# Other idle products and 18 idle elementwise operations behind the last product of a Fourier, mixer and channel-MLP kernel

## The chip, the cores and the metric

The kernel runs on one core of one Trainium2 chip. The metric is device time in microseconds (us) of one execution; a kernel's time is the median of several runs. The core has a matrix engine (TensorE, PE in the profile, with PEld for its weight loads), three elementwise engines (VectorE: DVE, ScalarE: ACT, GpSimd: POOL), SyncE (SP), which here only starts DMAs, and 16 DMA engines. [...]

## The reference

```python
def _attn_ref(x, w_r, w_i, b_r, b_i):            # x: 8 x 3136 x 256
    X = np.fft.rfft(x, axis=1)
    Yr = Xr @ w_r - Xi @ w_i + b_r
    Yi = Xr @ w_i + Xi @ w_r + b_i
    # soft threshold by 0.01 on Yr and Yi
    ...
    return np.fft.irfft(Y, n=x.shape[1], axis=1)

def _moe_ref(x, U, V, w_ch1, w_ch2):
    xt = x.transpose(0, 2, 1)
    h = xt @ U @ V                               # tokens, rank 32
    u = x + h.transpose(0, 2, 1)
    ch = np.maximum(u @ w_ch1, 0.0) @ w_ch2      # 256 -> 1024 -> 256
    return u + ch
```

The output is `_moe_ref` of `_attn_ref`, in fp32.

## The kernel before

The Fourier transforms of length 3136 = 49 x 64 are products with constant matrices, in stages over 8 batches. PSUM tiles are named after their stage: `psa` and `psb` transform, `psq` and `pst` mix the channels, `psc` and `psd` transform back, `psu`, `psp` and `psv` belong to the rank-32 token product. The channel MLP then runs over 49 windows of 512 tokens: `psx`, `psy` and `psz` hold its first layer, `pso0` and `pso1` its second. Most operands are split into a high and a low part (names ending in h and l) and multiplied in three products of type fp32r; VectorE, ScalarE and GpSimd make the splits, sums and ReLUs.

The work is recorded as a list of operations, and a planner (`_Program.order`) sets the order of each engine from costs and due times. `prog.trace` then issues them, so that each recorded operation has line 517 (the call in `trace`), whatever it is. Each engine runs its list in order; a wait is for a semaphore count of another engine or of its own. The last recorded operations are the second-layer products of window 47 (`pso`), two additions `xq<-xq,pso` and two transposes `os<-xq` on VectorE, one pair for each half of the 256 channels, and four DMAs `out_dram<-os`, two from SyncE and two from ScalarE.

Behind all of that, in program order, `more_idle` issues products whose results nobody reads. Before the change it issues on TensorE alone: 56 products over three PSUM tiles `psidle_0` to `psidle_2`, all with weights and columns out of `w1t`, a constant tile of 128 x 7168 fp32r values (the first layer's weights). They read 512 columns contiguously (5 with 128, 5 with 72 columns of weights), with a step of two (5), in pairs 256 columns apart (5), one pair again and again (5), in halves of the array (64 rows: 8 of 512, 8 of 256 columns and 6 of 64 in fp32), in quarters of it (64 rows and 64 weight columns: 4 of 256, in fp32), and shifted by one column (5). An fp32 product appears as two records in the trace, an fp32r product as one, so that 56 products are 66 records. Their line is 526, in the helper `mm`.

The name before `<-` in a row of the profile is the tile written, the names behind it the tiles read; `128x512` is partitions by elements.

Of the kernel before, what the change touches and what calls it, by code (L numbers as in the profile page):

```python
# [13 lines left out]
F32 = mybir.dt.float32  # L14
F32R = mybir.dt.float32r
U32 = mybir.dt.uint32
AF = mybir.ActivationFunctionType
ALU = mybir.AluOpType
# [498 lines left out]
            call(*[real(a) for a in op.args], **{k: real(a) for k, a in op.kw.items()})  # L517


def more_idle(nc, pool, w):  # L520

    o = [pool.tile([128, 512], F32, tag=f"psf.{k}", bufs=1, name=f"psidle_{k}") for k in range(3)]
    lhsT = w[:, 4096:4224]

    def mm(out, lhsT, rhs):
        nc.tensor.matmul(out, lhsT=lhsT, rhs=rhs, start=True, stop=True, skip_group_check=True)  # L526

    two = w[:, 0:1024].rearrange("p (n t) -> p t n", t=2)
    cross = w[:, 0:512].rearrange("p (t n) -> p n t", t=2)
    same = w[:, 0:2].unsqueeze(1).broadcast_to([128, 256, 2])  # L530
    for _ in range(5):
        mm(o[0], lhsT, w[:, 0:512])
    for _ in range(5):
        mm(o[0][:72], w[:, 4096:4168], w[:, 0:512])
    for _ in range(5):
        mm(o[0], lhsT, two[:, 0])
    for _ in range(5):
        mm(o[0].rearrange("p (n t) -> p n t", t=2), lhsT, cross)
    for _ in range(5):
        mm(o[0].rearrange("p (n t) -> p n t", t=2), lhsT, same)  # L540
    for n in (512, 256):
        for k in range(8):
            r = 64 * (k % 2)
            mm(o[1 + k % 2][:, :n], w[r : r + 64, 4096:4224], w[r : r + 64, 0:n])
    f = w.bitcast(F32)
    for k in range(6):
        r = 64 * (k % 2)
        mm(o[1 + k % 2][:, :64], f[r : r + 64, 4096:4224], f[r : r + 64, 0:64])
    for k in range(4):
        r, c = 64 * (k // 2), 64 * (k % 2)  # L550
        mm(o[1 + k // 2][c : c + 64, :256], f[r : r + 64, 4096:4160], f[r : r + 64, 0:256])
    for _ in range(5):
        mm(o[0], lhsT, w[:, 1:513])


@with_exitstack
def fft_mix_moe_kernel(
# [19 lines left out]
    nc = tc.nc  # L577
    prog = _Program()
    act, dve, pool, pe, dma = [prog.engine(e) for e in ("act", "dve", "pool", "pe", "sp")]
    const, dram = _Pool("const", 1), _Pool("dram", 1, "dram")  # L580
    ps_f, ps_m, ps_o = _Pool("ps_f", 3, "psum"), _Pool("ps_m", 1, "psum"), _Pool("ps_o", 1, "psum")
    fp, qp, mp = _Pool("fp", 2), _Pool("qp", 2), _Pool("mp", 1)
# [41 lines left out]
    w1t = const.tile([128, 7, 2, 512], F32R, name="w1t", tag="w1")  # L624
# [1078 lines left out]
    for w, prev, next_w in zip(turn_w, [None] + turn_w, turn_w[1:] + [None]):  # L1703
        b, j = divmod(w, NW)
# [18 lines left out]
        for g in range(2):  # L1723
            l1s = l1_chunks(w, g)
            new = l2_chunks(w, g)
            for k in range(4):
                for c in range(2):
                    n = WS * j + 8 * g + 2 * k + c
# [26 lines left out]
    make_identity(nc, ident.get())  # L1755
    with tc.manual_schedule():
        prog.trace(engines, ident.get())
        more_idle(nc, ps_f.real, w1t.get().rearrange("p a b c -> p (a b c)"))


def _dft_constants():
# [81 lines left out]
```

## Time and profile before

| | us |
|---|---|
| runs | 1695.21, 1695.93, 1697.87 |
| median | 1695.93 |
| profiled execution, its own time | 1696.02 |
| profiled execution, span | 1693.9 |
| mean granted TensorE clock | 1.000 |

The span runs from the first to the last instruction of the profiled execution, and its own time is 2.1 us longer. Times in a row of the timeline count from the start of the span. A row of the page's groups reads: line, engine, operation, tiles, shapes, count, then total busy us and mean ns of one, then the idle time of the engine before them and what ended it. A row of one tile's view has min, median and max ns of one, and the first and last start in us. A row of the timeline has start, length and what, and in brackets the idle time before it and its releaser; neighbours of one form are merged, with their count. Products are pipelined: the next starts before the last one ends, so that the step from start to start is shorter than one product's length.

### The profile page before, as it was taken

The page shows a single profiled execution, that of the slowest core. Times are in us where ns is not written, and L with a number is a line of the kernel's source. Part 1 is how long each engine was busy: PE and PEld are TensorE (multiplying, and loading weights), DVE is VectorE, ACT ScalarE, POOL GpSimd, SP SyncE. Part 2 cuts the span into 40 slices and gives each one's busy share as a digit, 9 for nine tenths or more (in the row PEclk, how much of TensorE's full clock was granted, in tenths as well). Part 3 has the DMA queues.
Part 4 walks back from the last instruction along what each step waited for, and adds up shares of the span by engine and source line. Part 5 has one row for each costly group of instructions (what it writes and reads, how often), then busy time and mean ns, then how long its engine had stood idle before and what let it go on. Part 6 is the DMA issues. An engine that isn't in the chain of part 4 may idle for free.

```text
span 1693.9 us, 31590 instructions
## 1 busy us (share of the span) xinstructions
PE 1685.3 (99%) x11170; PEld 1517.5 (90%) x11170; DVE 1323.8 (78%) x2487; ACT 1015.1 (60%) x2187; POOL 574.9 (34%) x502
## 2 busy tenths in 40 slices
PE   9999999999999999999999999999999999999999
PEld 6979989999898999999988989999989999998888
DVE  6798898589856989678866788768985689766774
ACT  4766776466665765456666666555666566554442
POOL 2312553133533443133344444123343233211221
DMA  9863444223653444313464344422465233410221
GB/s 256 243 225 92 139 124 129 86 80 108 173 163 109 129 141 118 110 51 89 133 198 124 118 142 112 133 69 73 118 167 160 63 104 104 119 59 18 69 66 26
DMA packets 243448, 200.64 MB, mean 118 GB/s; under 512 B 131386, under 2 KB 192608, under 8 KB 243292
## 3 DMA queue, kind: packets, MB, share of 16 engines
q1 hardware_dynamic: 240654, 197.77, 40.5%
q8 instruction: 89, 1.46, 0.4%
q10 hardware_dynamic: 2638, 0.86, 0.2%
q14 instruction: 67, 0.55, 0.1%
HBM read 121.36 MB, written 77.20 MB: 117 GB/s over the span
## 4 chain that ended last, share of the span: by engine, by line
PE 97%; DMA 2%; DVE 1%; ACT 0%; POOL 0%; issue 0%; SPq 0%; DVEq 0%
PE pso L517 32%; PE psy L517 18%; PE psx L517 8%; PE psq L517 7%; PE psd L517 7%; PE psb L517 5%; PE psa L517 5%; PE psz L517 4%; PE psc L517 4%; PE pst L517 4%; PE psv L517 1%; PE psidle L526 1%; DMA xx<-in_x_dram 0%; DMA fb<-in_fb_dram 0%; DMA zt<-zd 0%; DMA fas<-in_fa_dram 0%
## 5 line engine op out<-in xcount | busy, mean ns | idle before, releaser
L517 PE MATMUL pso<-rh,w2t 128*128 128x512 f32 x1568 | 433.5, 398 | 0.0
L517 PEld LDWEIGHTS pso<-rh,w2t 128*128 128x128 f32 x1568 | 275.3, 188 | 44.8
L517 PE MATMUL pso<-rl,w2t 128*128 128x512 f32 x784 | 246.7, 396 | 0.0
L517 DVE SCALAR_TENSOR_TENSOR ys<-tb,rl 64x256 f32<-64x256 f32 x350 | 197.3, 564 | 12.2 <-ACT rl L517 6.8
L517 POOL TENSOR_TENSOR yl<-ys,yh 128x512 fp32r<-128x512 f32 (+1 forms) x101 | 136.8, 1354 | 190.7 <-ACT yh L517 173.1
L517 POOL TENSOR_TENSOR xl<-xt,xh 98x512 fp32r<-98x512 f32 x96 | 130.6, 1360 | 204.7 <-ACT xh L517 190.4
L517 PEld LDWEIGHTS pso<-rl,w2t 128*128 128x128 f32 x784 | 147.4, 188 | 35.3
L517 DVE SCALAR_TENSOR_TENSOR rl<-s,rh 128x512 fp32r<-128x512 f32 x196 | 156.5, 805 | 5.1 <-ACT rh L517 2.9
L517 ACT ACTIVATE rh<-s 128x512 fp32r<-128x512 f32 x196 | 121.6, 629 | 57.6 <-DVE s L517 56.3
L517 POOL TENSOR_TENSOR tl<-ts,th 128x256 fp32r<-128x256 f32 x88 | 71.0, 806 | 203.8 <-ACT th L517 144.2
L517 PE MATMUL psq<-wmt,xsh 128*128 128x256 f32 (+1 forms) x704 | 130.3, 282 | 0.0
L517 PE MATMUL psy<-odh,w1t 128*128 128x256 f32 x784 | 126.2, 283 | 0.0
L517 DVE TENSOR_TENSOR v<-v,psy 128x512 f32<-128x512 f32 x98 | 67.1, 685 | 72.9 <-ACT v L517 63.1
L517 PEld LDWEIGHTS psy<-odh,w1t 128*128 128x128 f32 x784 | 113.5, 189 | 10.0
L517 PEld LDWEIGHTS psq<-wmt,xsh 128*128 128x128 f32 (+1 forms) x704 | 112.0, 188 | 5.3 <-issue 0.2
L517 PE MATMUL psd<-dt,zt 98*128 98x130 f32 x896 | 115.0, 275 | 0.5 <-DMA dt<-dud 0.5
L517 PEld LDWEIGHTS psd<-dt,zt 98*128 98x128 f32 x896 | 110.9, 190 | 4.6 <-issue 0.7
L517 ACT ACTIVATE xsh<-psb 128x256 fp32r<-128x256 f32 (+1 forms) x176 | 60.5, 381 | 89.7 <-PE psb L517 87.4
L517 ACT ACTIVATE xq<-psd 128x196 f32<-128x196 f32 x256 | 82.0, 332 | 48.0 <-PE psd L517 37.3
L517 DVE TENSOR_TENSOR pa<-pa,psd 128x64 f32<-128x64 f32 x248 | 54.1, 218 | 68.1 <-ACT xq L517 59.1
L517 ACT ACTIVATE v<-psx 128x512 f32<-128x512 f32 x98 | 58.6, 598 | 76.8 <-PE psx L517 67.3
L517 POOL TENSOR_TENSOR ocl<-xq,och 128x256 fp32r<-128x256 f32 x47 | 37.8, 804 | 195.0 <-ACT och L517 194.9
(217 smaller groups left out, 4296.0 us busy)
## 6 DMA issues: line engine op xcount, KB each, us to landing
zt<-zd SPq DMA_DIRECT2D x128, 196.0 KB
zd<-zs SPq DMA_DIRECT2D x192, 128.0 KB
out_dram<-os SPq DMA_DIRECT2D x190, 128.0 KB
t<-gd SPq DMA_DIRECT2D x168, 128.0 KB
xt<-in_x_dram SPq DMA_DIRECT2D x100, 196.0 KB
gd<-gs SPq DMA_DIRECT2D x96, 196.0 KB
fb<-in_fb_dram SPq DMA_DIRECT2D x96, 128.0 KB
vw<-vd SPq DMA_DIRECT2D x96, 128.0 KB
```

The lines of the kernel that those rows point to most:

```text
L517: call(*[real(a) for a in op.args], **{k: real(a) for k, a in op.kw.items()})
L526: nc.tensor.matmul(out, lhsT=lhsT, rhs=rhs, start=True, stop=True, skip_group_check=True)
```

## The change

`more_idle` gets the SBUF pool `mp` too, and its products are others: 75 in place of 56, 24 of them in fp32, so 99 records. They are, in order: 3 contiguous; 16 that read pairs of columns 4, 16, 64 or 128 apart (4 of each, all 512 columns in all); 8 that read runs of 4 or of 16 columns in turn from the two halves of the 512; 4 with two runs of 256 columns, 1024 apart; 4 with four columns in turn, 128 and 256 apart, whose output is permuted as well; 9 of 256 columns in pairs 128 apart; 5 of 256 contiguous columns; 16 in quarters of the array, 49 rows and 64 weight columns, of 81 columns, and 8 such of 512, in fp32; 2 contiguous again. The quarters write `psidle_1` and `psidle_2`, all others `psidle_0`.

Behind them stand 18 elementwise operations, in two equal passes over 512 columns: on VectorE three additions of `w1t` and `psidle_0` (contiguous; PSUM read with a step of two; SBUF read with a step of two), on ScalarE four copies (out of PSUM contiguous and with a step of two, out of SBUF with a step of two, into SBUF with a step of two), and on GpSimd two additions of two parts of `w1t` (contiguous; one part with a step of two). Each engine writes one tile of its own, in the slots `sv.0`, `sv.1` and `sv.2` that the first layer's sums (`s`, `v`) used before.

```diff
-def more_idle(nc, pool, w):
+def more_idle(nc, pool, mp, w):
 
     o = [pool.tile([128, 512], F32, tag=f"psf.{k}", bufs=1, name=f"psidle_{k}") for k in range(3)]
     lhsT = w[:, 4096:4224]
+    f = w.bitcast(F32)
 
     def mm(out, lhsT, rhs):
         nc.tensor.matmul(out, lhsT=lhsT, rhs=rhs, start=True, stop=True, skip_group_check=True)
 
...
+    for _ in range(3):
+        mm(o[0], lhsT, w[:, 0:512])
+    for st in (4, 16, 64, 128):
+        r = w[:, 0:512].rearrange("p (b t n) -> p b n t", t=2, n=st)
+        for _ in range(4):
+            mm(o[0].rearrange("p (b n t) -> p b n t", t=2, n=st), lhsT, r)
+    for st in (4, 16):
+        r = w[:, 0:512].rearrange("p (t b n) -> p b t n", t=2, n=st)
+        for _ in range(4):
+            mm(o[0].rearrange("p (b t n) -> p b t n", t=2, n=st), lhsT, r)
+    r = w[:, 0:2048].rearrange("p (t n) -> p t n", t=2)[:, :, 0:256]
+    for _ in range(4):
+        mm(o[0].rearrange("p (t n) -> p t n", t=2), lhsT, r)
+    r = w[:, 0:512].rearrange("p (t b a) -> p a b t", t=2, b=2)
+    for _ in range(4):
+        mm(o[0].rearrange("p (b a t) -> p a b t", t=2, b=2), lhsT, r)
+    r = w[:, 0:256].rearrange("p (t n) -> p n t", t=2)
+    for _ in range(9):
+        mm(o[0][:, 0:256].rearrange("p (n t) -> p n t", t=2), lhsT, r)
     for _ in range(5):
+        mm(o[0][:, 0:256], lhsT, w[:, 0:256])
+    for k in range(16):
+        r, c = 64 * (k // 2 % 2), 64 * (k % 2)
+        mm(o[1 + k // 2 % 2][c : c + 64, 81 * (k // 4) : 81 * (k // 4) + 81], f[r : r + 49, 4096:4160], f[r : r + 49, 0:81])
+    for k in range(8):
+        r, c = 64 * (k // 2 % 2), 64 * (k % 2)
+        mm(o[1 + k // 2 % 2][c : c + 64], f[r : r + 49, 4096:4160], f[r : r + 49, 0:512])
+    for _ in range(2):
         mm(o[0], lhsT, w[:, 0:512])
...
+    a, b, c, d = [mp.tile([128, 512], F32, tag=f"sv.{k}", bufs=1, name=f"idle_{k}") for k in range(4)]
+    s0, s1 = f[:, 0:512], f[:, 512:1024]
+    even = s0.rearrange("p (n t) -> p t n", t=2)
+
+    def both(x):
+        return x.rearrange("p (t n) -> p t n", t=2)
+
+    for _ in range(2):
+        nc.vector.tensor_tensor(out=a, in0=s0, in1=o[0], op=ALU.add)
+        nc.vector.tensor_tensor(out=both(a), in0=both(s1), in1=o[0].rearrange("p (n t) -> p t n", t=2), op=ALU.add)
+        nc.vector.tensor_tensor(out=both(a), in0=even, in1=both(o[0]), op=ALU.add)
+        nc.scalar.activation(b, o[0], AF.Copy)
+        nc.scalar.activation(both(b), o[0].rearrange("p (n t) -> p t n", t=2), AF.Copy)
+        nc.scalar.activation(both(b), even, AF.Copy)
+        nc.scalar.activation(b.rearrange("p (n t) -> p t n", t=2), both(s1), AF.Copy)
+        nc.gpsimd.tensor_tensor(out=c, in0=s0, in1=s1, op=ALU.add)
+        nc.gpsimd.tensor_tensor(out=both(c), in0=even, in1=both(s1), op=ALU.add)
```

Each engine's list is the same as before up to its end. VectorE's end, before and after (what it waits for in brackets; `idle_0` is the tile `a`):

```order
 L517 TENSOR_TENSOR xq_7_16_19055<-xq_7_16_19055,pso_47_1_20951 128x16x32 [waits PE_49]
 L517 STREAM_TRANSPOSE os_47_21061<-xq_7_16_19055 128x16x32 [waits DVE_49]
-L1838 UNCONDITIONAL_BRANCH
+L567 TENSOR_TENSOR idle_0_21147<-w1t_982,psidle_0_21069 128x512 [waits PE_49]
+L568 TENSOR_TENSOR idle_0_21147<-w1t_982,psidle_0_21069 128x512 [waits DVE_49]
+L569 TENSOR_TENSOR idle_0_21147<-w1t_982,psidle_0_21069 128x512 [waits DVE_49]
+L567 TENSOR_TENSOR idle_0_21147<-w1t_982,psidle_0_21069 128x512 [waits DVE_49,Activation_49]
+L568 TENSOR_TENSOR idle_0_21147<-w1t_982,psidle_0_21069 128x512 [waits DVE_49]
+L569 TENSOR_TENSOR idle_0_21147<-w1t_982,psidle_0_21069 128x512 [waits DVE_49]
+L1860 UNCONDITIONAL_BRANCH
```

Six additions stand where the list ended. By the counts of the built program, the first waits for TensorE's last product, the fourth for ScalarE's second new copy, and each of the others for the one before it.

ScalarE's end (`idle_1` is the tile `b`):

```order
 L517 DMA out_0_dram<-os_47_21061 32x16x64 [waits DMAHW0_49,DVE_49]
 L517 DMA out_0_dram<-os_47_21061 32x16x64 [waits DMAHW3_49]
-L1838 UNCONDITIONAL_BRANCH
+L570 ACTIVATE idle_1_21148<-psidle_0_21069 128x512 [waits DVE_49,PE_49,Activation_49]
+L571 ACTIVATE idle_1_21148<-psidle_0_21069 128x512 [waits Activation_49]
+L572 ACTIVATE idle_1_21148<-w1t_982 128x512 [waits Activation_49]
+L573 ACTIVATE idle_1_21148<-w1t_982 128x2x256 [waits Activation_49]
+L570 ACTIVATE idle_1_21148<-psidle_0_21069 128x512 [waits DVE_49,Activation_49]
+L571 ACTIVATE idle_1_21148<-psidle_0_21069 128x512 [waits Activation_49]
+L572 ACTIVATE idle_1_21148<-w1t_982 128x512 [waits Activation_49]
+L573 ACTIVATE idle_1_21148<-w1t_982 128x2x256 [waits Activation_49]
+L1860 UNCONDITIONAL_BRANCH
```

Eight copies stand behind the last output DMAs. By the counts, the first `L570` waits for VectorE's third new addition, the second for its sixth.

GpSimd's end (`idle_2` is the tile `c`):

```order
 L517 TENSOR_TENSOR obl_47_20819<-xq_7_16_19055,obh_47_20800 128x512 [waits PE_49,Activation_49]
 L517 TENSOR_TENSOR odl_47_20862<-tt_47_20758,odh_47_20853 128x512 [waits PE_49,Activation_49]
-L1838 UNCONDITIONAL_BRANCH
-L1838 ISA [waits barrier_Pool_Activation_PE_DVE_SP_gather]
+L574 TENSOR_TENSOR idle_2_21149<-w1t_982 128x512 [waits DVE_49]
+L575 TENSOR_TENSOR idle_2_21149<-w1t_982 128x512 [waits Pool_49]
+L574 TENSOR_TENSOR idle_2_21149<-w1t_982 128x512 [waits Pool_49]
+L575 TENSOR_TENSOR idle_2_21149<-w1t_982 128x512 [waits Pool_49]
+L1860 UNCONDITIONAL_BRANCH
+L1860 ISA [waits barrier_Pool_Activation_PE_DVE_SP_gather]
```

Four additions stand between the last real one and the closing barrier. The first waits for the VectorE operation that last used slot `sv.2`, the second `rl<-s` of window 47's first half, and for no product.

More of the change, by code (lines that the diff above doesn't have):

```diff
@@ L517, in trace @@
             call(*[real(a) for a in op.args], **{k: real(a) for k, a in op.kw.items()})
-def more_idle(nc, pool, w):
+def more_idle(nc, pool, mp, w):
     o = [pool.tile([128, 512], F32, tag=f"psf.{k}", bufs=1, name=f"psidle_{k}") for k in range(3)]
     lhsT = w[:, 4096:4224]
+    f = w.bitcast(F32)
     def mm(out, lhsT, rhs):
         nc.tensor.matmul(out, lhsT=lhsT, rhs=rhs, start=True, stop=True, skip_group_check=True)
-    two = w[:, 0:1024].rearrange("p (n t) -> p t n", t=2)
-    cross = w[:, 0:512].rearrange("p (t n) -> p n t", t=2)
-    same = w[:, 0:2].unsqueeze(1).broadcast_to([128, 256, 2])
-    for _ in range(5):
-        mm(o[0], lhsT, w[:, 0:512])
[L533 to L553, printed above, removed]
@@ L1757, in fft_mix_moe_kernel @@
         prog.trace(engines, ident.get())
-        more_idle(nc, ps_f.real, w1t.get().rearrange("p a b c -> p (a b c)"))
+        more_idle(nc, ps_f.real, mp.real, w1t.get().rearrange("p a b c -> p (a b c)"))
 def _dft_constants():
```

## The prediction

> **What bounds the kernel now.** I read the page first, then the chain of waits, then the timeline of the last 18 us, because every edit sits behind the last product that the output needs.
>
> ```profile
> span 1693.9 us, 31590 instructions
> PE 1685.3 (99%) x11170; PEld 1517.5 (90%) x11170; DVE 1323.8 (78%) x2487; ACT 1015.1 (60%) x2187; POOL 574.9 (34%) x502
> PE 97%; DMA 2%; DVE 1%; ACT 0%; POOL 0%; issue 0%; SPq 0%; DVEq 0%
> ```
>
> TensorE is busy for 99% of the span and carries 97% of the chain. Two pieces end that chain (start, length, what); the timeline shows what stands beside them, and the DMA view's busy row when the output lands:
>
> ```profile
> 1675.81 6.31 PE pso L517 x27
> 1682.12 10.92 PE psidle L526 x61
> ```
>
> ```profile
> 1681.03 0.40 PE L517 MATMUL pso<-rl,w2t 128*128 128x512 f32 x1
> ...
> 1681.53 0.69 DVE L517 TENSOR_TENSOR xq<-xq,pso 128x512 f32<-128x512 f32 x1 [5.06 <-PE pso L517]
> 1681.96 11.08 PE L526 MATMUL psidle<-w1t 128*128 128x512 f32 x66
> 1682.26 0.71 DVE L517 STREAM_TRANSPOSE os<-xq 128x512 f32<-128x512 f32 x1
> 1683.58 0.71 DVE L517 STREAM_TRANSPOSE os<-xq 128x512 f32<-128x512 f32 x1
> 1684.32 0.93 ACTq L517 DMA_DIRECT2D out_dram<-os  x2
> ```
>
> ```profile
> DMA  0100000000000005789200000000000000000000
> ```
>
> The idle products start at 1681.96, with no gap behind the last real one, and end at 1681.96 + 11.08 = 1693.04. The span ends 0.9 later. VectorE writes the last output tile until 1684.3, its DMAs are issued by 1685.3, and the last row, 40 slices of 0.6 us from 1676, shows their packets over by about 1688. So the real work ends 5 us before the idle products do, and the end of the span is TensorE's idle block plus 0.9. Any time added to that block, or put in a row behind it, is paid in full; nothing is left to hide it.
>
> **The products, price by price.** These rows give the step from one start to the next, which is what a queue of products costs (the 0.4 us of one product overlaps its neighbours).
>
> ```profile
> 1681.73 2.73 PEld L526 LDWEIGHTS psidle<-w1t 128*128 128x128 f32 x12
> 1685.16 0.21 PEld L526 LDWEIGHTS psidle<-w1t 128*128 128x128 f32 x1 [0.24 <-issue]
> 1685.61 0.21 PEld L526 LDWEIGHTS psidle<-w1t 128*128 128x128 f32 x1 [0.24 <-issue]
> 1686.51 1.94 PEld L526 LDWEIGHTS psidle<-w1t 128*128 128x128 f32 x9 [0.24 <-issue]
> 1665.31 1.40 PE psy L517 x12
> 1690.46 0.50 PE L526 MATMUL psidle<-w1t 64*128 64x64 f32 x6
> 1690.80 0.87 PE L526 MATMUL psidle<-w1t 64*128 64x64 f32 x10
> 1691.01 0.45 PE L526 MATMUL psidle<-w1t 64*64 64x256 f32 x4
> 1691.27 0.40 PE L526 MATMUL psidle<-w1t 64*64 64x256 f32 x4
> 1691.60 0.49 PE L526 MATMUL psidle<-w1t 128*128 128x512 f32 x1
> 1691.93 1.11 PE L526 MATMUL psidle<-w1t 128*128 128x512 f32 x4
> ```
>
> Weight loads mark the steps. Twelve loads in 2.73 us, the last lasting 0.19, belong to the contiguous products: (2.73 - 0.19) / 11 = 0.231 us. The lone loads at 1685.16 and 1685.61 belong to products whose columns step by two: 0.45 us, twice as much. The nine from 1686.51 belong to products that read columns in pairs, 256 apart or the same pair again: (1.94 - 0.19) / 8 = 0.219 us. Twelve real products of 256 columns take 1.40: 0.117 us. In quarters of the array, four fp32 products run at once, each in two passes: the first passes start at 1691.01, the second at 1691.27, the next full product at 1691.60. A second pass of 256 columns and the return to the full array take 0.33, the first pass 0.26 with 0.05 of weight load in it, so a pass costs 0.21 / 256 = 0.84 ns a column, and the return 0.11. The last pairs of products before them step by (1690.80 - 1690.46) / 3 = 0.11 (the row of six is three pairs), and entering the quarters took 1691.01 - 1690.80 = 0.21, so 0.1 extra; the first full product afterwards took 0.33 to its successor, again 0.1 extra.
>
> The old block of 11.08 goes. The new one, in its order:
>
> - 3 contiguous products: 3 x 0.231 = 0.69.
> - 16 with pairs of columns 4, 16, 64 and 128 apart. No row has these distances. Their ends are 0.219 (pairs 256 apart) and 0.45 (step of two), so 3.50 to 7.20. I take 3.50: it is the same form of read, alternating between two runs, and only the distance differs.
> - 8 with runs of 4 and 16 columns in turn: runs are nearer to contiguous, 0.231, so 1.85 (ends as above, up to 3.6).
> - 4 with two runs of 256: 0.92.
> - 4 with four columns in turn: 0.88 by the pairs' row, up to 1.80.
> - 9 + 5 of 256 columns: 14 x 0.117 = 1.64.
> - 16 quarter products of 81 columns: 4 rounds x 2 passes x 81 x 0.84 ns = 0.54; 8 of 512 columns: 2 x 2 x 512 x 0.84 ns = 1.72; entry, first load and return 0.1 + 0.05 + 0.11 = 0.26.
> - 2 contiguous: 0.33 to the second start and 0.40 for the last product's own length: 0.73.
>
> Sum 12.73, against 11.08: the block grows by 1.65 and ends at 1694.69.
>
> [...]
>
> **The elementwise operations.** In the order of instructions the first addition on VectorE waits for the last idle product, whose bank it reads; ScalarE's first copy waits for VectorE's third addition, since both read that bank; VectorE's second three wait for ScalarE's second copy; ScalarE's second four wait for those. So twelve of the fourteen stand in one row: 3 additions, 2 copies, 3 additions, 4 copies. Only the first L572 and L573 run beside something (VectorE's second three). Each also waits for its predecessor on its engine, since all write one tile.
>
> ```profile
> L517 DVE TENSOR_TENSOR v<-v,psy 128x512 f32<-128x512 f32 x98 | 67.1, 685 | 72.9 <-ACT v L517 63.1
> L517 ACT ACTIVATE v<-psx 128x512 f32<-128x512 f32 x98 | 58.6, 598 | 76.8 <-PE psx L517 67.3
> L517 ACT ACTIVATE dm<-dw x8: 660/672/687, 47.4 to 116.1; 128x512 f32<-128x512 f32 x8
> L517 DVE SCALAR_TENSOR_TENSOR dm<-dw,dm x8: 681/683/693, 51.5 to 122.3; 128x512 uint32<-128x512 uint32 x8
> L517 ACT ACTIVATE rh<-s x196: 612/632/657, 132.3 to 1673.8; 128x512 fp32r<-128x512 f32 x196
> L517 DVE STREAM_TRANSPOSE t0t<-psa x16: 1007/1019/1072, 9.5 to 23.3; 128x512 f32<-128x512 f32 x16
> L517 DVE STREAM_TRANSPOSE os<-xq x96: 661/702/714, 163.8 to 1683.6; 128x512 f32<-128x512 f32 x96
> L517 ACT ACTIVATE vh<-v x2: 1148/1160/1172, 55.8 to 58.9; 96x512 fp32r<-96x512 f32 x2
> 1670.35 0.69 DVE L517 TENSOR_TENSOR v<-v,psy 128x512 f32<-128x512 f32 x1 [1.77 <-PE psy L517]
> 1671.07 0.63 ACT L517 ACTIVATE rh<-v 128x512 fp32r<-128x512 f32 x1 [0.91 <-DVE v L517]
> ```
>
> An addition of SBUF and PSUM takes 0.685, a copy out of PSUM 0.598. `dw` is read with a step of two in SBUF: 0.683 on VectorE, no more than contiguous, and 0.672 on ScalarE, 0.04 above the 0.632 of `rh<-s`. A write with a step of two (L573) has no row: I take 0.63, as contiguous, with the 1.16 of `vh`, whose read steps by 32, as its upper end. A step of two in PSUM (L568, L571) has none either: the lower end is the contiguous 0.685 and 0.598; the upper is bounded by `t0t`, read from PSUM with a step of 16, which lasts 0.32 longer than `os`, and by `vh`, 0.53 longer than `rh`. I take the lower end, since the nearest rows by step, both of `dw`, are nearly free. A handover costs 1671.07 - (1670.35 + 0.69) = 0.03; I give each of eleven 0.035 and TensorE's to VectorE 0.10, as from the end of the last product of the first `pso` half (1681.03 + 0.40) to the addition at 1681.53.
>
> Six additions 6 x 0.685 = 4.11; four PSUM copies 4 x 0.598 = 2.39; one read and one write with a step 0.67 + 0.63 = 1.30; handovers 0.49: 8.29 us behind the last product.
>
> **GpSimd's four additions** read only weights, and their first wait is for a VectorE result, `rl<-s`, long before the end.
>
> ```profile
> 1657.46 1.28 POOL L517 TENSOR_TENSOR odl<-tt,odh 128x512 fp32r<-128x512 f32 x1 [2.65 <-ACT odh L517]
> 1663.66 1.47 DVE L517 SCALAR_TENSOR_TENSOR rl<-s,rh 128x512 fp32r<-128x512 f32 x2
> L517 DVE SCALAR_TENSOR_TENSOR rl<-v,rh x98: 649/685/2291, 134.4 to 1671.7; 128x512 fp32r<-128x512 f32 x98
> 1673.74 1.40 DVE L517 SCALAR_TENSOR_TENSOR rl<-s,rh 128x512 fp32r<-128x512 f32 x2
> 1677.29 0.63 PE L517 MATMUL pso<-rl,w2t 128*128 128x512 f32 x2
> ```
>
> GpSimd is free from 1658.7, so they start near 1665.1 (1663.66 + 1.47) and, at 1.28 each, end near 1670.4; their cover is TensorE's own work. VectorE operations on two SBUF tiles can stretch from 0.685 to 2.29 beside GpSimd; the next such starts at 1671.7. Should slow steps push GpSimd into it, 1.6 is lost at most, while the `rl` ready at 1675.14 is first read at 1677.29: 2.15 of slack. Price 0; with the cover gone, it would show as a TensorE wait there.
>
> **Sum.** 1.65 + 8.29 = +9.94 on a span of 1693.9. This execution's own time is 1696.02, so 1705.96; the median shown, 1695.93, is 0.09 lower. I say 1705.9, slower by 0.6%. About 0.2% (3.4 us) is what a measurement here can tell from no change.
>
> **Rivals.**
> - *PSUM read with a step of two is slow* (0.22). L568 and L571 stand twice each in the row: 2 x 0.32 + 2 x 0.53 = +1.7, so 1707.6. For it speaks `t0t`, against it `dw`. [...]
> - *Pairs closer than 256 columns pay like the step of two* (0.15). If only 4 and 16 apart, 8 x 0.23 = +1.8: 1707.7; if all pairs and the fours, 20 x 0.23 = +4.6: 1710.5. For it: 0.45 exists at the smallest step. Against it: 0.219 for pairs.
> - *VectorE and ScalarE do not take turns* (0.04). Then ScalarE's eight alone set the tail: 4 x 0.598 + 2 x 0.67 + 2 x 0.63 + 0.35 = 5.3, 3.0 less: 1702.9. Against it stand the waits in the order. [...]
> - *The other side: the elementwise work runs beside the products* (0.03). That is so if the first addition's wait is met before the two closing products rather than by the last one; from the point where it is met 8 us earlier, only the block's 1.65 is paid: 1697.6, within 0.2%. Against it: those two write the bank that it reads.
>
> **Chances and range.** The forecast has 0.56. From 1704.5 (1.4 below, for handovers, quarters and the spread of runs) to 1709.6 (slow PSUM and near pairs together, 1705.9 + 3.5, and a little) the range leaves out the last two rivals, all pairs slow, and some noise, under 2 in 10. Slower by over 0.2%: 0.96; within: 0.03; faster: 0.01.
>
> **What would show it.** The last idle product ends near 1694.7; its group has 99 records in place of 66; pair products step by about 0.22 in the weight loads; a first addition starts about 0.1 later, and one of VectorE and ScalarE is always busy until about 1703; the first L570 is put down to VectorE; the chain ends in ACT instead of PE. GpSimd's four lie before 1672 and no `pso` product waits. I am wrong if both engines overlap behind the last product, if a PSUM step takes 1 us, or if the pairs' loads are 0.45 apart.

## The result, and the profile after

The changed kernel took 1708.34 us (median of three runs, 1707.62 to 1710.32), where the kernel before took 1695.93: a ratio of 1.0073, with a 95% interval of 1.0050 to 1.0096. The prediction was 1705.9 with a range of 1704.5 to 1709.6, so it is slower by about as much as was said, with the median 2.4 us over the number.

The page of the kernel after, profiled in the run of 1710.32: span, engines, and the shares of the chain that ended last.

```profile
span 1708.5 us, 31677 instructions
PE 1689.8 (99%) x11203; PEld 1520.1 (89%) x11203; DVE 1327.6 (78%) x2493; ACT 1020.4 (60%) x2195; POOL 579.4 (34%) x506
PE 95%; DMA 2%; DVE 1%; ACT 1%; SPq 0%; issue 0%; POOL 0%; DVEq 0%; ACTq 0%
```

ACT, which had no share of the chain, now has 1%: the last operation is ScalarE's. The timeline of the kernel after shows the end (start, length, engine, line, what; in brackets the idle time before it and what ended that):

```profile
1685.97 13.00 PE L527 MATMUL psidle<-w1t 128*128 128x512 f32 x99
...
1699.01 0.69 DVE L567 TENSOR_TENSOR idle<-w1t,psidle 128x512 f32<-128x512 f32 x1 [10.71 <-PE psidle L527]
1699.73 0.69 DVE L568 TENSOR_TENSOR idle<-w1t,psidle 128x512 f32<-128x512 f32 x1
1700.45 0.69 DVE L569 TENSOR_TENSOR idle<-w1t,psidle 128x512 f32<-128x512 f32 x1
1701.26 0.60 ACT L570 ACTIVATE idle<-psidle 128x512 f32<-128x512 f32 x1 [21.49 <-DVE idle L569]
...
1702.51 0.69 DVE L567 TENSOR_TENSOR idle<-w1t,psidle 128x512 f32<-128x512 f32 x1 [1.37 <-ACT idle L571]
...
1706.69 0.66 ACT L573 ACTIVATE idle<-w1t 128x512 f32<-128x512 f32 x1
```

From the first idle product to the end of the span there were 1693.9 - 1681.96 = 11.9 us before; now there are 1708.5 - 1685.97 = 22.5. So this tail grew by 10.6, in three pieces: the products last 13.00 in place of 11.08 (+1.92); the row of elementwise operations runs from 1699.01 to 1706.69 + 0.66 = 1707.35 (8.34; counted from the end of the products +8.38); and from the last operation to the end of the span it is 1.15, where it was 0.86 (+0.29).

The other part of this profile's difference lies ahead of the tail: the idle products start at 1685.97 in place of 1681.96. Part of that can be seen at the start of the program. These two rows are the stretch from 10 to 20 us, of before and then of after (stretch, its length, busy time and instructions of PE, PEld, DVE, ACT and POOL, the granted TensorE clock, the DMA share, GB/s):

```profile
10.00:20.00 10.00, 10.00 (x27) 4.59 (x26) 10.00 (x12) 1.26 (x2) 1.41 (x2) 1.00 1.05 284
```

```profile
10.00:20.00 10.00, 10.00 (x18) 4.00 (x18) 7.27 (x8) 0.63 (x1) 1.29 (x1) 0.72 0.82 210
```

In this execution the granted clock was 0.72 in that stretch and TensorE got through 18 products in place of 27. Whether that came with the change or with the run is the first question for the experiments.

### The profile page after: what moved, and what is told of

Read it like the earlier page. It is cut to its first block, busy times and chain, and to the rows that moved or that the text cites. A ratio compares the mean times of both kernels' runs of the same rounds, so it can differ in the third digit from the quotient of the medians.

```text
span 1708.5 us, 31677 instructions
## 1 busy us (share of the span) xinstructions
PE 1689.8 (99%) x11203; PEld 1520.1 (89%) x11203; DVE 1327.6 (78%) x2493; ACT 1020.4 (60%) x2195; POOL 579.4 (34%) x506
## 4 chain that ended last, share of the span: by engine, by line
PE 95%; DMA 2%; DVE 1%; ACT 1%; SPq 0%; issue 0%; POOL 0%; DVEq 0%; ACTq 0%
PE pso L517 32%; PE psy L517 17%; PE psx L517 8%; PE psq L517 7%; PE psd L517 7%; PE psa L517 5%; PE psb L517 5%; PE psz L517 4%; PE psc L517 4%; PE pst L517 4%; PE psv L517 1%; PE psidle L527 1%; DMA zt<-zd 1%; SPq L517 0%; DMA xx<-in_x_dram 0%
```

## Experiments

Every kernel ran beside the kernel before on the same chip; the ratios are against those runs.

**The change once more.** The kernel is the changed one as it is.

> The changed kernel once more, beside the kernel before on the same chip. Tail theory (the change costs only what stands behind the last real product: +1.92 in the idle products, 8.35 for the row of elementwise operations, 0.27 in the closing barrier, 10.5 in all): about 1706.5 us where the kernel before takes 1696.0, a ratio of 1.0062, and the idle products start at the same time in both, within the spread of the kernel before. Start rival (the added instructions also make the part before the idle products later, by the 1.9 us that the first measurement had over the tail): about 1708.3, a ratio of 1.0073, in every round, with idle products that start about 2 us later than in the kernel before.

Measured: 1707.25 us (five runs) against 1695.87 (fifteen), ratio 1.0067, interval 1.0054 to 1.0080. The timeline of this run:

```profile
1684.25 13.00 PE L527 MATMUL psidle<-w1t 128*128 128x512 f32 x99
...
1704.97 0.66 ACT L573 ACTIVATE idle<-w1t 128x512 f32<-128x512 f32 x1
```

The products last 13.00 again, and the tail is 1706.7 - 1684.25 = 22.45, as in the first profile within 0.1 us. The start of the tail moved by 1.7 us between two executions of one and the same kernel. The stretch from 10 to 20 us of this run:

```profile
10.00:20.00 10.00, 10.00 (x27) 4.59 (x26) 10.00 (x12) 1.16 (x2) 1.30 (x1) 1.00 0.97 279
```

The granted clock is 1.00 there and TensorE gets through 27 products, as in the kernel before, so the low clock of that stretch is not a fixed part of the change: it came in one execution and not in the other. Over the whole execution, the three runs of the first measurement have a mean granted clock of 0.995 to 0.997, and the five here 0.998. The interval of the time holds both theories' ratios. What tells more is the kernel before itself: in the 47 runs of it that stand beside all experiments here its span goes from 1692.5 to 1697.9 us, with a mean of 1695.1. In 19 of them the mean granted clock is under 1.000, and these have a mean span of 1696.6, against 1694.1 for the others. The eight runs of the changed kernel have a mean span of 1706.3, 11.2 more, with an uncertainty of about 0.6 (their standard deviation of 1.5 over the root of eight). The tail explains 10.5 to 10.6 of it; the rest is about one such uncertainty. So a cost of the change ahead of the tail is not excluded, but nothing shows one, and the surplus of the first three runs is as large as what the kernel before varies by.

**Products alone.** The new products, without the block from `a, b, c, d = ...` on.

```
-    a, b, c, d = [mp.tile([128, 512], F32, tag=f"sv.{k}", bufs=1, name=f"idle_{k}") for k in range(4)]
...
-        nc.gpsimd.tensor_tensor(out=both(c), in0=even, in1=both(s1), op=ALU.add)
```

> The new idle products without the 18 elementwise operations. Tail theory: the idle block ends the span again, 1.9 us later than before: 1697.9, ratio 1.0011. If the start rival holds and it is the added products that delay the start: 1699.8. If the products of the prediction had the sizes that it gave them: 1697.6.

Measured: 1698.19, ratio 1.0011, interval 1.0002 to 1.0020. The expectation is met. The timeline of this run:

```profile
1682.65 13.00 PE L527 MATMUL psidle<-w1t 128*128 128x512 f32 x99
```

The idle products last 13.00 here as well and end at 1695.65, 0.85 ahead of the end of the span.

**Elementwise operations alone.** The old products, with the same 18 operations behind them.

```
     for _ in range(5):
         mm(o[0], lhsT, w[:, 1:513])
+    a, b, c, d = [mp.tile([128, 512], F32, tag=f"sv.{k}", bufs=1, name=f"idle_{k}") for k in range(4)]
...
+        nc.gpsimd.tensor_tensor(out=both(c), in0=even, in1=both(s1), op=ALU.add)
...
```

> The old idle products with the 18 new elementwise operations behind them. Tail theory: the row of 8.35 us with 0.27 for the barrier is all that is added: 1704.6, ratio 1.0051. This and the products alone must add up to the whole change (1.9 + 8.6 = 10.5). Start rival, with the elementwise operations as the cause: 1706.5.

Measured: 1705.80, ratio 1.0053, interval 1.0040 to 1.0066. The timeline of this run (the lines of the operations are L563 to L569 in this file):

```profile
1681.69 11.08 PE L526 MATMUL psidle<-w1t 128*128 128x512 f32 x66
...
1692.81 0.69 DVE L563 TENSOR_TENSOR idle<-w1t,psidle 128x512 f32<-128x512 f32 x1 [8.79 <-PE psidle L526]
...
1700.48 0.66 ACT L569 ACTIVATE idle<-w1t 128x512 f32<-128x512 f32 x1
```

The row lasts 1700.48 + 0.66 - 1692.81 = 8.33 behind an unchanged block of 11.08. The two halves of the change give 1.0011 and 1.0053, together 1.0064, and the whole gave 1.0067: they add up, as the tail says.

**No idle work.** The call of `more_idle` is left out.

```
-        more_idle(nc, ps_f.real, w1t.get().rearrange("p a b c -> p (a b c)"))
```

> No idle work at all behind the last product. Tail theory: the end is then set by the last output tile: its last transfers land about 5 us before the old idle block ended (the trace of before has the packets over at about 1688, the span ends 0.9 after the last work): about 1691, ratio 0.997. Rival: the end of the program has to wait for something that the idle products covered (the completion of the output's transfers), and little is gained: 1694 to 1696.

Measured: 1691.49, ratio 0.9969, interval 0.9956 to 0.9981, as the tail theory had it. The last output tile sets the end now (timeline of this run; its span is 1687.6):

```profile
1682.82 0.93 ACTq L517 DMA_DIRECT2D out_dram<-os  x2
```

From these issues to the end it is 4.8 us. With the idle products this transfer was hidden, by the 5 us that the prediction read off the profile.

**No turns.** ScalarE's copies out of PSUM read another bank than VectorE's additions, the tile `psidle_1` in place of `psidle_0`.

```
-        nc.scalar.activation(b, o[0], AF.Copy)
-        nc.scalar.activation(both(b), o[0].rearrange("p (n t) -> p t n", t=2), AF.Copy)
+        nc.scalar.activation(b, o[1], AF.Copy)
+        nc.scalar.activation(both(b), o[1].rearrange("p (n t) -> p t n", t=2), AF.Copy)
```

> ScalarE's four copies out of PSUM read the second idle bank, which only the quarter products fill, instead of the bank that VectorE's additions read. Theory of the turns (the row is VectorE and ScalarE waiting for each other, since both read one bank): ScalarE starts after the quarter products, about 0.7 us before the last product ends, runs its eight in 4 x 0.597 + 2 x 0.667 + 2 x 0.660 + 7 x 0.03 = 5.25 us beside VectorE's six (6 x 0.69 + 0.15 = 4.3), and the end comes 3.5 to 4.0 us earlier than in the changed kernel: tail +6.5 to +7.0 over before, about 1702.7, ratio 1.004; the chain has one engine alone behind the products. Rival (the row is long because each of these operations waits for something else, such as its own engine's write): the end stays within 1 us of the changed kernel's, 1706.5.

Measured: 1702.71, ratio 1.0034, interval 1.0022 to 1.0045: 3.3 thousandths, or 5.6 us, below the ratio of the whole change. The timeline of this run:

```profile
1682.52 13.00 PE L527 MATMUL psidle<-w1t 128*128 128x512 f32 x99
...
1694.95 0.60 ACT L570 ACTIVATE idle<-psidle 128x512 f32<-128x512 f32 x1 [18.64 <-PE psidle L527]
1695.55 0.69 DVE L567 TENSOR_TENSOR idle<-w1t,psidle 128x512 f32<-128x512 f32 x1 [10.71 <-PE psidle L527]
...
1699.56 0.66 ACT L573 ACTIVATE idle<-w1t 128x512 f32<-128x512 f32 x1
```

ScalarE starts on the quarter products, now put down to PE in place of VectorE, and runs beside VectorE. The tail is 1701.3 - 1682.52 = 18.8, 3.7 less than with turns, inside the 3.5 to 4.0 expected (the rest of the 5.6 is within the two intervals). So 3.7 us of the row come from the turns that the two engines take over one bank.

**Beside the products.** The same operations are issued behind the first three idle products, and the other products write the two other banks.

```
     for _ in range(3):
         mm(o[0], lhsT, w[:, 0:512])
+    a, b, c, d = [mp.tile([128, 512], F32, tag=f"sv.{k}", bufs=1, name=f"idle_{k}") for k in range(4)]
+    ...
     for st in (4, 16, 64, 128):
...
-            mm(o[0].rearrange("p (b n t) -> p b n t", t=2, n=st), lhsT, r)
+            mm(o[1].rearrange("p (b n t) -> p b n t", t=2, n=st), lhsT, r)
```

> All 18 elementwise operations are issued after the first three idle products, and the other 96 products write the other two banks. Theory (the 8.35 us are paid only because the wait for the last product puts them behind TensorE's end): the row still lasts about 8.3 us by its turns, but runs from about 1685 (when VectorE has written the last output tile) to 1693.5, beside products that end at about 1695; the tail is the products' 1.9 us alone: 1697.9, ratio 1.0011. Rival (VectorE and ScalarE beside TensorE stretch each other, or the products wait): 1699 or more, with additions longer than 0.69 us or products further apart.

Measured: 1698.26, ratio 1.0010, interval 1.0001 to 1.0019, the same as the products alone. The timeline of this run (the operations are L539 to L545):

```profile
1684.11 13.00 PE L527 MATMUL psidle<-w1t 128*128 128x512 f32 x99
...
1686.36 0.65 DVE L539 TENSOR_TENSOR idle<-w1t,psidle 128x512 f32<-128x512 f32 x1
...
1694.12 0.69 ACT L545 ACTIVATE idle<-w1t 128x512 f32<-128x512 f32 x1
```

The row takes 8.45 us, at 1686.36 to 1694.81, beside products that last 13.00 as ever. This is the prediction's rival for the other side, made to come true: what cost 8.3 us behind the last product costs nothing beside it.

**Twelve additions on GpSimd.** Each of the two forms is issued three times in a row.

```
-        nc.gpsimd.tensor_tensor(out=c, in0=s0, in1=s1, op=ALU.add)
+        for _ in range(3):
+            nc.gpsimd.tensor_tensor(out=c, in0=s0, in1=s1, op=ALU.add)
...
```

> Twelve additions on GpSimd instead of four. In the changed kernel's profile the four lie at 1669.2 to 1674.7 and VectorE's next operation on two SBUF tiles starts at 1675.75 with a 2.15 us margin. Theory of the cover (GpSimd's work costs nothing while it stays clear of such VectorE operations, and at most the stretch beyond the margin when it does not): twelve end at about 1685, the rl operations at 1675.75, 1677.76 and 1679.80 stretch from 0.69 to between 1 and 2.3 us each, and the real products end 0 to 2 us later: 1706.5 to 1708.5, with a wait of TensorE for rl in the trace if it is over 0. Rival (GpSimd does not touch VectorE here): every rl stays at 0.69 us, and the time is the changed kernel's.

Measured: 1705.47 (four runs), ratio 1.0051, interval 1.0035 to 1.0066: not slower than with four, and under the 1706.5 to 1708.5 that was expected. The timeline shows that the cover was nearly used up (PEld is the weight load):

```profile
1671.44 0.85 DVE L517 SCALAR_TENSOR_TENSOR rl<-v,rh 128x512 fp32r<-128x512 f32 x1 [0.70 <-ACT rh L517]
...
1673.59 3.51 DVE L517 SCALAR_TENSOR_TENSOR rl<-s,rh 128x512 fp32r<-128x512 f32 x2
...
1677.15 0.30 PEld L517 LDWEIGHTS pso<-rl,w2t 128*128 128x128 f32 x2 [0.43 <-DVE rl L517]
```

The two `rl<-s` that took 1.40 in the kernel before take 3.51 beside GpSimd's additions, and a weight load then waits 0.43 for `rl`. The starts of the `pso<-rl` products around it are 1675.59, 1677.15 and 1678.66, where 1.41 apart is usual there, so TensorE lost 3.07 - 2.82 = 0.25. Eight more additions cost no more than that; the four of the change are clear of it.

**A probe.** In the idle place, twelve products each of eleven forms, each form behind four small ones, and elementwise operations with larger steps.

> A probe in the idle place: twelve products each of eleven forms of read and write, four small fp32 products between the forms, then VectorE and ScalarE operations that read PSUM with steps of 1, 2, 4, 16 and 64 and ScalarE copies that write SBUF with these steps, two of each. Disputed: four columns in turn took 0.27 us a product where 0.22 was predicted. Theory W (the written places cost it: pairs that are written in turn to two places 256 columns apart): the form with a plain read and this write steps by 0.27, the one with this read and a plain write by 0.22, and runs of four and of 32 written in turn lie between 0.23 and 0.27. Theory R (the four-column read costs it): the other way round. Pairs of columns 2, 8 and 256 apart in the read, written plainly: 0.216 each if the distance never matters, 0.45 for the nearest ones if it does. Step of two read: 0.45. Elementwise: a step of two in PSUM is free (0.686 on VectorE, 0.597 on ScalarE); theory: larger steps in PSUM are free too, and the 1.0 us of the old t0t<-psa transposes is their write; rival: steps from 16 on cost about 0.3 us more.

It ran once, in 1750.13 us; only its rows are used. The timeline of the probe, row by row: contiguous; four columns in turn as in the change; that read with a plain write; a plain read with that write; runs of four written in turn (runs of 32 gave the same); pairs 2 columns apart; pairs 8 apart (two forms with pairs 256 apart gave the same); a step of two.

```profile
1681.57 2.92 PE L526 MATMUL psidle<-w1t 128*128 128x512 f32 x12
...
1685.14 3.63 PE L526 MATMUL psidle<-w1t 128*128 128x512 f32 x12
...
1689.42 3.62 PE L526 MATMUL psidle<-w1t 128*128 128x512 f32 x12
...
1693.68 2.99 PE L526 MATMUL psidle<-w1t 128*128 128x512 f32 x12
...
1697.33 3.01 PE L526 MATMUL psidle<-w1t 128*128 128x512 f32 x12
...
1704.65 3.01 PE L526 MATMUL psidle<-w1t 128*128 128x512 f32 x12
...
1708.31 2.84 PE L526 MATMUL psidle<-w1t 128*128 128x512 f32 x12
...
1715.27 5.65 PE L526 MATMUL psidle<-w1t 128*128 128x512 f32 x12
```

The first has no small products ahead of it; the others compare with one another. Theory R holds: the read of four columns in turn costs the 0.6 us per twelve, (3.62 - 3.01) / 12 = 0.05 each over runs, and the scattered write costs nothing, 2.99. Pairs 8 or more columns apart are faster than a plain read (2.84 against 2.99), pairs 2 apart are not (3.01), and a step of two takes nearly twice as long (5.65). What in the four-column read costs it, the two distances or the third level of the pattern, was not tried.

The groups of the probe's elementwise operations (VectorE's reads of PSUM with all five steps; ScalarE's; then ScalarE's SBUF writes with steps of 1, 2, 4, 16 and 64; minimum, median, maximum in ns):

```profile
L564 DVE TENSOR_TENSOR idle<-w1t,psidle x10: 686/686/689, 1724.4 to 1730.9; 128x512 f32<-128x512 f32 x10
L572 ACT ACTIVATE idle<-psidle x10: 597/597/597, 1731.7 to 1737.4; 128x512 f32<-128x512 f32 x10
```

```profile
L575 ACT ACTIVATE idle<-w1t x2: 629/629/629, 1738.0 to 1738.7; 128x512 f32<-128x512 f32 x2
L575 ACT ACTIVATE idle<-w1t x2: 657/657/657, 1739.3 to 1740.0; 128x512 f32<-128x512 f32 x2
L575 ACT ACTIVATE idle<-w1t x2: 1100/1100/1101, 1740.7 to 1741.9; 128x512 f32<-128x512 f32 x2
L575 ACT ACTIVATE idle<-w1t x2: 1057/1058/1059, 1743.0 to 1744.1; 128x512 f32<-128x512 f32 x2
L575 ACT ACTIVATE idle<-w1t x2: 1065/1066/1066, 1745.2 to 1746.3; 128x512 f32<-128x512 f32 x2
```

Reading PSUM with the steps tried, up to 64, cost nothing on either engine: 0.686 on VectorE and 0.597 on ScalarE throughout. A step in ScalarE's SBUF write is nearly free at two (0.657 for 0.629) and costs 0.43 to 0.47 us at 4, 16 and 64.

**Pairs in the real work.** The probe and the change both say that a product of 512 columns takes 0.216 in pairs and about 0.23 in a row, so the second layer of the kernel before was given pairs, with its idle block left as it was.

```
-            r = [t[:, j].rearrange("p k n -> p (k n)") for t in m_state[w, g, i]]
+            r = [t[:, j].rearrange("p k n -> p n k") for t in m_state[w, g, i]]
...
-                    po[h],
+                    po[h].rearrange("p (n k) -> p n k", k=2),
...
-                out=x[:, h], in0=x[:, h], in1=po[h].rearrange("p (i q) -> p i q", q=32), op=ALU.add
+                out=x[:, h].rearrange("p (k a) q -> p k a q", k=2),
+                in0=x[:, h].rearrange("p (k a) q -> p k a q", k=2),
+                in1=po[h].rearrange("p (a q k) -> p k a q", k=2, q=32),
+                op=ALU.add,
```

> The idle block of before, but the 2352 real products of the second layer (pso) read their 512 columns in pairs 256 apart, as the idle pairs do, and the additions that take the result out of PSUM read it with a step of two. The order of the instructions is that of before. Theory (a product in pairs takes 0.216 us wherever it stands, and PSUM reads with a step of two are free): 2352 x (0.2333 - 0.216) = 41 us less, 1656, ratio 0.976, if TensorE stays the bound; the xq<-xq,pso additions stay at 0.68 us. Rival (in the real work the weight loads or the waits for rl set the step, or reads by pairs collide with what VectorE and ScalarE write): a gain under 15 us, with pso products that still step by 0.23 or with new waits of TensorE.

Measured: 1662.43 against 1697.22, ratio 0.9794, interval 0.9775 to 0.9814: 35 us less, of 41 expected. Four second-layer products in the kernel before, and in this one, with what follows them:

```profile
905.79 1.09 PE L517 MATMUL pso<-rh,w2t 128*128 128x512 f32 x4
906.72 0.63 PE L517 MATMUL pso<-rl,w2t 128*128 128x512 f32 x2
```

```profile
901.92 1.03 PE L517 MATMUL pso<-rh,w2t 128*128 128x512 f32 x4
902.78 0.59 PE L517 MATMUL pso<-rl,w2t 128*128 128x512 f32 x2
```

Four take (906.72 - 905.79) / 4 = 0.233 each before and (902.78 - 901.92) / 4 = 0.215 now, so the step came out as said. In the two profiles the stretch from the first to the last second-layer product shrank by 36 us, from 1546.3 (135.2 to 1681.5) to 1510.3 (138.4 to 1648.7), so most of the missing 6 us lie inside it, where TensorE stood idle 1.6 us more; the rest was not traced to a place.

**Pairs and no idle work.** The same, without the call of `more_idle`.

> The same second layer in pairs, and no idle work at the end. Theory: the gain of the pairs and the 4.4 us that leaving out the idle work gave are paid at different places and add up: 1651.5, ratio 0.974. Rival (see the pairs alone): 1677 to 1691.

Measured: 1654.34, ratio 0.9753, interval 0.9735 to 0.9771. The two gains add up: the difference to the run before is 4.1 thousandths, with intervals that let it be the 2.6 expected.

**Pairs in both layers.** The first layer reads pairs too; the banks are put back in order as they are read, and one VectorE operation of each group is split in two.

```
-                    rhs=r[rk],
+                    rhs=r[rk].rearrange("p (t n) -> p n t", t=2),
...
-            relu(rh[:, :, 0], rl[:, :, 0], y)
+            act.activation(split2(rh[:, :, 0]), turned(y), AF.Relu)
+            for n in range(2):
+                dve.scalar_tensor_tensor(
...
```

> As the run before, and the 4116 products of the first layer (256 columns each) read pairs 128 apart too; ScalarE and VectorE put the columns back in order as they read PSUM (steps of two), for which one VectorE operation in each group becomes two halves. Theory: idle products of 256 columns stepped by 0.112 in pairs and by 0.117 to 0.120 otherwise; 4116 x 0.005 = 20 us less, about 1631, ratio 0.962, if VectorE (78% busy) keeps up. Rival (VectorE and ScalarE, with more operations and less time, become the bound, or a step of two in PSUM beside busy engines costs): 1650 or more, with TensorE waiting for rl and rh.

Measured: 1657.02, ratio 0.9767, interval 0.9751 to 0.9783: 2.7 us slower than with the second layer alone, where 20 us less were expected. The products themselves did gain: in the profile six first-layer products pass in 0.67 us, in place of 0.69 to 0.72. The second layer's row of one tile's view shows where the time went (first and last start), first with the second layer alone and then in this run:

```profile
L517 PE MATMUL pso<-rh,w2t x1568: 377/379/464, 134.9 to 1644.1; 128*128 128x512 f32 x196
```

```profile
L517 PE MATMUL pso<-rh,w2t x1568: 377/379/483, 143.1 to 1646.3; 128*128 128x512 f32 x196
```

The first second-layer product starts 8.2 us later here. The first product of the first layer starts 9.3 us later already (135.4 against 126.1), so this loss lies ahead of every product that was changed. In the page's row of the granted clock, in tenths over 40 slices of 41 us, the slice from 83 to 124 us has 7 in this profile, where it has 9 (0.9 or more) with the second layer alone, and the mean clock is 0.992 or 0.993 in all four runs, against 0.999 in all four of the other kernel. Why it fell is not shown: the order of TensorE's products differs there, but the profile of the run with pairs in the second layer and the old idle work, whose order is that of before, has 8 in the same slice. From the first to the last second-layer product it is 1509.2 us with the second layer alone and 1503.2 here, 6.0 of the 20 us. From 130 to 1600 us TensorE stands idle 13.2 us, against 1.2 with the second layer alone. The largest of its waits from 200 to 1650 us (total, times, longest), in this run and in the one with the second layer alone:

```profile
PE pso L517 <- DVE rl L517: 2.7, 5, 0.7
PE psc L517 <- ACT oah L517: 1.4, 1, 1.4
PE psy L517 <- DVE v L517: 1.2, 3, 0.6
```

```profile
PE psd L517 <- DVE pa L517: 0.3, 1, 0.3
```

So the late start (8.2) and the added idle time (12.0) make up 20 of the 22.7 us that are missing. Most of the waits are for VectorE and ScalarE; a few are for GpSimd and DMAs. Two causes were left for them: the split operations, or the pairs and steps themselves.

**Pairs where no operation is split.** Of the first layer only the products of the banks `x` and `z`, which no relu reads.

```
-            l1(w, g, x, 3, "t1", True)
+            l1(w, g, x, 3, "t1", True, two=True)
...
-            l1(w, g, x, 6, "b22", False, True)
+            l1(w, g, x, 6, "b22", False, True, two=True)
...
-            l1(w, g, z, 1, "b21", True, True)
+            l1(w, g, z, 1, "b21", True, True, two=True)
```

> As the run with the second layer in pairs and no idle work, and of the first layer only the three of seven products whose banks (psx, psz) are read without a relu, so that no VectorE operation is split: 1764 products in pairs 128 apart. Theory (the first layer in pairs lost its gain to the split VectorE operations and the waits of TensorE for rl that they brought): 1764 x 0.006 = 10 us less than with the second layer alone, a ratio near 0.969 in place of 0.975. Rival (reading PSUM with a step of two and three dimensions, or the shorter steps themselves, bring TensorE's waits): 0.974 or more, with TensorE waiting for rl again.

Measured: 1643.79 against 1696.99, ratio 0.9689, interval 0.9676 to 0.9703: the 10 us came, with no wait of TensorE over 0.4 from 200 us on and a mean clock of 0.999 in all five runs. This is the fastest of all kernels here, 3.1% below the kernel before. The pairs and steps of these three products brought no such waits, so the waits of the run before came with the other four products and the split operations; these two were not separated, and neither was what lowered the clock there.

## Why the prediction was right, and what it missed

- *The bound.* The prediction said that TensorE's idle block ends the program, with 5 us of the real work's end hidden below it. Without the block the end came 4.4 us earlier; with a longer block alone it came later by about what the block grew (2.3 for 1.92, with an interval of 0.3 to 3.4).
- *The products*, said 12.73, measured 13.00 or 13.01 in the six profiles that have them all. The sixteen in pairs came out at 0.216 for 0.219 at all four distances. The mis-sized term is the four columns in turn: priced by the pairs' row at 0.219, they stepped by 0.277 in the block (the probe has them 0.05 above plain runs), so the four of them were 0.23 us dearer than said. That term had its upper end at 0.45 in the prediction, and the truth lay between. The eight with runs in turn took 1.96 for 1.85, and the pairs a little less than said. Of the twelve weight loads that the prediction gave to contiguous products, two belong to products with a step of two; in the trace each of the twelve starts within 0.01 us of the product ahead of it, so that their spacing is that of contiguous products and 0.231 stands.
- *The elementwise row*, said 8.29, measured 8.38 as the prediction counted, from the end of the products. The order told that VectorE and ScalarE would take turns, and taking the turns away gave 3.7 us back. A step of two in PSUM was priced at nothing and cost nothing (0.69 for L568 as for L567, 0.60 for L571 as for L570). The write with a step of two was 0.66 for 0.63.
- *GpSimd's four*, said 0: in the profile after they lie at 1669.2 to 1674.7, clear of VectorE's next work on two SBUF tiles at 1675.75, and twelve of them would still cost only about 0.25.
- *The sum*, said +9.94: the tail grew by 10.6. Of the 0.65 missing, 0.27 is in the products, 0.09 in the row, and 0.29 in the way from the last operation to the end of the span, which the prediction kept at 0.9. That way was 1.15 in the profile after and 1.16 with the elementwise operations alone, 0.85 with the products alone, 1.19 with the row beside the products, and 0.79 with twelve additions on GpSimd; what sets it stays open.
- *The time.* The median lies 2.4 us over the number, and the tail holds only 0.65 of that. The other 1.8 us lie ahead of the tail, where two executions of one kernel differ by as much; the lower mean clock of the three runs (0.995 to 0.997, against 0.998 later) points to their start, but no run shows what the 1.8 came from. The prediction set its sum against one execution and let the spread of runs widen its range only downwards: the medians of the five groups of runs of the kernel before go from 1695.87 to 1697.41, and with the tail's 10.6 they give 1706.5 to 1708.0. Its range reached to 1709.6 for slow PSUM and near pairs, neither of which came; that this width also held the 1.8 us is partly luck.
- *The rivals.* PSUM with a step of two is not slow. The row that spoke for it, `t0t`, also writes SBUF, with a step of 128; PSUM reads with a step of 16 cost VectorE nothing in the probe (0.686), so they are not shown to be the source of its 0.32; whether that write is, was not tried. Near pairs are not slow (0.216 at 4 columns apart), though 2 columns apart they lose their advantage (3.01 for twelve, against 2.84). No turns and work beside the products do what the prediction gave them, and both were made to happen: 1702.7 for 1702.9, and 1698.3 for 1697.6.

## What to carry to other kernels

Work behind the last product was paid in full here, while the same work beside the products was free: 8.3 us or nothing, by which bank it reads and when its wait is met. Before costing a row of small operations on two engines, look in the order for a bank that both read; the turns over it were worth 3.7 of 10.6 us here. And a price seen in an idle block can be worth more than the block: reading columns in pairs in the second layer took 35 us off, and 53 with three of the first layer's seven products in pairs too and the idle work left out.

## What the runs showed of the hardware

- A product of 512 fp32r columns takes 0.216 us from start to start where it reads pairs of columns 4, 16, 64 or 128 apart (the changed kernel), 0.215 with pairs 256 apart (the second layer in pairs), 0.231 contiguously and 0.45 with a step of two (the kernel before), and 0.28 with four columns in turn (the changed kernel). Twelve with pairs 8 apart took 2.84 us, with pairs 2 apart 3.01, and with a plain read 2.99 (the probe). In the written forms that the probe tried, where the result goes in PSUM made no difference (2.99 to 3.01 for twelve).
- Reading PSUM with steps of 1, 2, 4, 16 and 64 took VectorE 0.686 us and ScalarE 0.597 at every step (the probe). ScalarE's SBUF write took 0.63 in a row, 0.66 with a step of two, and 1.06 to 1.10 with steps of 4, 16 and 64; why it turns slow at four was not shown.
- An operation of VectorE on two SBUF tiles took about 1.75 us beside GpSimd's additions, on average of two (twelve additions on GpSimd), in place of 0.70 in the kernel before.
- The granted clock was 0.72 in the stretch from 10 to 20 us of one execution of the changed kernel, with 18 products in place of 27, and 1.00 with 27 products in another; from 83 to 124 us it was 0.7 to 0.8 in the profile with both layers in pairs. What lowered it was not shown.
